# The order of the steps in an attention slot: value products directly behind the scores, all transposes together

## The chip, the cores and the metric

The kernel runs on one core of one Trainium2 chip. The metric is the time of one execution on the device, in microseconds (us). Lower is better. The core has a matrix engine (TensorE, PE in the profile, whose weight loads are listed as PEld), a vector engine (VectorE, DVE), a scalar engine (ScalarE, ACT), a general engine (GpSimd, POOL) and an engine that issues transfers (SyncE, SP). Each engine works through its own list of instructions in order; semaphores hold an instruction until what it needs is there.

## The reference

A threshold attention is followed by a feed-forward layer with squared ReLU. All inputs of the attention are float32; the two weight matrices arrive as float64.

```python
# q, k, v: (8, 8, 576, 64), tau = 0.02
scores = (1.0 / np.sqrt(64)) * np.matmul(q, k.transpose(0, 1, 3, 2))
thresh = np.max(scores, axis=-1, keepdims=True) - tau
scores = np.where(scores >= thresh, scores, -1000000000.0)
scores = scores - np.max(scores, axis=-1, keepdims=True)
attn = np.exp(scores)
attn = attn / (np.sum(attn, axis=-1, keepdims=True) + 1e-09)
attn_out = np.matmul(attn, v)

# (B, H, S, D) -> (B*S, H*D) = (4608, 512); w_in: (512, 2048), w_out: (2048, 512)
x = attn_out.transpose(0, 2, 1, 3).reshape(4608, 512)
h = np.maximum(x @ w_in, 0.0)
out = h * h @ w_out
```

## The kernel before

**Stages.** The attention comes first (0 to about 663 us), then the hidden layer for nine groups of 512 tokens, then the output layer for the same nine groups. Both layers use a fast matrix multiplication of two levels (seven products in place of eight, twice), whose sums of weights are made on GpSimd during the attention. The change touches the attention alone.

**Head pairs and blocks.** Two heads of one batch entry form a pair; there are 32. A pair has 576 queries, in four blocks of 128 and one of 64 (`t` = 0 to 4, `FULL` = 4), which makes 160 blocks in `slots`. In a full block the two heads stand side by side along the free dimension; in the block of 64 they share the partitions, so it has half the work on the other engines.

**The order of the work is written out by hand.** `slot(n)` (lines 558 to 584) is called for n = -3 to 159. Each call issues the next steps of several blocks, as a software pipeline; the order of the calls in it is the order of the instructions on each engine. The steps of one block:

- `ahead(n + 3, 0)` and `ahead(n + 3, 1)`: the scores of block n + 3. The first takes a score buffer from `sc_pool` (two buffers) and makes the last 64 keys' scores of both heads (line 340; nothing for a block of 64 queries). The second makes the main 512 keys' scores, each head on half of the rows of the array (line 355). Below, these two are called K and S.
- `stage` and `second` move the generator `softmax` on: first head's maximum, second head's maximum and threshold (lines 366 and 371), the exponentials (378) for block n + 2; the two selections with their sums (383), the addition of 1e-9 (387), the reciprocal (389) and the normalisation on GpSimd (398) for block n + 1. A block of 64 queries has one head's worth of these, and `second` skips it.
- `turn_part(n - 1, ...)`: the transposes of the weights of block n - 1, in three parts: "w" for the second head's 512 keys (nothing for a block of 64), "W" for the first head's (both line 439, four transposes each, copied out of the matmul banks by ScalarE at lines 441 or 444), and "R" for the remaining 64 keys of both heads (line 414).
- `values_and_load(n - 2)`: the value products of block n - 2 (lines 469 and 474, each head on half of the columns of the array). Below, V. With the last block of a pair it also issues loads of a later pair's values.
- R puts its transpose into the same bank as V's result (the queue `pending`); its copies (lines 418 to 427) take both out on ScalarE, and the result goes to DRAM at the next `ask()`. In the slot where n - 1 is a pair's first block, R also makes the last transpose for the next pair's queries and keys (line 317), with two more copies (320, 321), two small ones on GpSimd (324), and the loads of a further pair on the SP queue.
- `turn_step(n, 0)` and `turn_step(n, 1)`: only in slots where n is a multiple of 5 (and not for the last pair), four transposes of the next pair's queries and four of its keys (line 306, copies at 311 and 309). Below, q and k.
- `sums_step()`: one sum of weights on GpSimd (lines 130 and 133), in slots 35 to about 78 and 111 to 154. Below, Q.
- `fetch` and `convert1` to `convert6`: load and conversion of one piece of a weight matrix, begun in slots 0, 2, ... 30 and 76, 78, ... 106 (`starts`). They are spread over the slots from three before to four after.

**Banks.** The transposes and the value products take their banks of matmul results from one pool, `b_pool`, with two buffers, in turn (lines 888 and 890). A new tile in a buffer waits for the last reader of the tile before. R takes no bank of its own where V has left one in `pending`.

On TensorE a slot before the change is: w, q, V, R, W, K, k, S.

Of the kernel before, what the change touches and what calls it, by code (L numbers as in the profile page):

```python
# [48 lines left out]
def kernel(  # L49
# [26 lines left out]
    B, H, S, D = q.shape  # L76
# [92 lines left out]
    def weight(m):  # L169
        return weight_tile(*chunks[m][0:3])  # L170

    def fetch(m):
        if m is None:
            return
        src = chunks[m][3]
        three = (lambda t: t.rearrange("p (k o) -> p k o", k=4)) if m < 16 else (lambda t: t)
        if src.dtype == FP32:
            nc.sync.dma_start(out=three(weight(m)[:, :]), in_=src)
            return
        raw = sb.tile([P, 2 * WC], I32, tag="raw", bufs=4, name="raw")  # L180
        nc.sync.dma_start(out=three(raw[:, :]), in_=src.bitcast(I32))
        raws[m] = raw
# [10 lines left out]
    def pick(t, k):  # L193
        return t.rearrange("p (n two) -> p n two", two=2)[:, :, k]

    def convert1(m):
        if m not in raws:
            return
        lo, hi = pick(raws[m], 0), pick(raws[m], 1)
        a = pick(sb.tile([P, 2 * WC], I32, tag="a", bufs=2, name="a"), 0)  # L200
        nc.scalar.activation(out=a.bitcast(FP32), in_=hi.bitcast(FP32), func=AF.Abs)
        parts[m] = (lo, hi, a)
        raws.pop(m)

    def convert2(m):
        if m in parts:
            lo = parts[m][0]
            nc.scalar.activation(out=lo, in_=lo.bitcast(U32), func=AF.Copy, bias=0.0, scale=2.0**-29)

    def convert3(m):  # L210
        if m not in parts:
            return
        a = parts[m][2].bitcast(FP32)
        low, high = (0x38000000, 0x47EFFFFF)
        nc.gpsimd.tensor_scalar(
            out=a, in0=a, scalar1=as_float(high), scalar2=as_float(low), op0=ALU.min, op1=ALU.max
        )

    def convert4(m):
        if m not in parts:  # L220
            return
        lo, hi, a = parts[m]
        nc.vector.tensor_scalar(
            out=a, in0=a, scalar1=3, scalar2=0x3FFFFFFF, op0=ALU.logical_shift_left, op1=ALU.bitwise_and
        )

    def convert5(m):
        if m not in parts:
            return
        lo, hi, a = parts[m]  # L230
        nc.vector.scalar_tensor_tensor(
            out=hi, in0=hi, scalar=-(1 << 30), in1=a, op0=ALU.bitwise_and, op1=ALU.bitwise_or
        )

    def convert6(m):
        if m not in parts:
            return
        lo, hi, _ = parts.pop(m)
        nc.gpsimd.tensor_tensor(out=weight(m)[:, :].bitcast(I32), in0=hi, in1=lo, op=ALU.add)
# [47 lines left out]
    def load_v(i):  # L287
        b, hp = pairs[i]
        h = 2 * hp
        va = sb.tile([P, 2, FULL, D], FP32, tag="va", bufs=2, name="va")  # L290
        vd = vdiag[i % 2]
        nc.sync.dma_start(out=va[:, :, :, :], in_=v[b, h : h + 2, 0:MAIN, :].rearrange("j (p t) d -> p j t d", p=P))
        for j in range(2):
            nc.sync.dma_start(out=vd[ds(j * D, D), ds(j * D, D)], in_=v[b, h + j, MAIN:S, :])
        loaded_v[i] = (va, vd)

    def turn(i):

        qn, kn, rn = loaded.pop(i)
        qT = sb.tile([P, S], FP32, tag="qT", bufs=2, name="qT")  # L300
        kT = sb.tile([P, S], FP32, tag="kT", bufs=2, name="kT")
        turning[i] = (qT, kT, rn)
        for nat, to in ((qn, qT), (kn, kT)):
            pt = bank([P, FULL, P], "pqk")
            for t in range(FULL):
                nc.tensor.transpose(pt[:, t, :], nat[:, t, :], ident[:, :])
            flat, to = pt[:, :, :].rearrange("p t m -> p (t m)"), to[:, 0:MAIN]
            if nat is kn:
                nc.scalar.copy(to, flat)
            else:  # L310
                nc.scalar.activation(out=to, in_=flat, func=AF.Identity, scale=qscale[:, :])  # L311
            yield
# [18 lines left out]
    def scores_rest(i, t):  # L331

        sc = sc_pool.tile([P, 3 * BANK], FP32, tag="sc", name="sc")
        if t < FULL:
            qT, _ = turned[i]
            to = sc[:, MAIN:S]
            to = bass.AP(tensor=to.tensor, offset=to.offset, ap=[to.ap[0], [2 * BANK - S, 2], [1, REST]])
            nc.tensor.matmul(to, qT[:, ts(t, P)], kdiag[i % 2][:, :], start=True, stop=True)  # L340
        return sc

    def scores(i, t, sc):

        qT, kT = turned[i]
        m = BLK[t]  # L350
        for k0, n in ((0, MAIN),) if t < FULL else ((0, MAIN), (MAIN, REST)):
            for j in range(2):
                rows = ds(j * D, D)
                to = sc[rows, ds(k0, n)] if t == FULL else sc[:, ds(j * 2 * BANK, n)]
                nc.tensor.matmul(to, qT[rows, ds(t * P, m)], kT[rows, ds(k0, n)], start=True, stop=True)  # L355
# [94 lines left out]
    def turn_part(n, part):  # L450

        if n < 0:
            return
        if n not in rows_of:
            transposes(n)
        rows_of[n][part]()

    def values(i, t):

        wT, wR = weights.pop((i, t)), rests.pop((i, t))  # L460
        va, vd = loaded_v[i]
        n = BLK[t]
        pt = bank([P, 3, P], "pvR")
        pv = pt[:, 0, 0:n]

        for c in range(FULL):
            for j in range(2):
                rows = ds(j * D, D)
                nc.tensor.matmul(  # L469
                    pv[rows, :], va[:, j, c, :], wT[:, j, c, 0:n], start=(c == 0), stop=False, skip_group_check=True  # L470
                )
        for j in range(2):
            rows = ds(j * D, D)
            nc.tensor.matmul(
                pv[rows, :], vd[:, rows], wR[:, 0:n], start=False, stop=True, skip_group_check=True
            )
        pending.append((pt, n, NB * i + t))
# [12 lines left out]
    def turn_step(n, at):  # L490
        i, left = divmod(n - TURN_AT[at], NB)
        i += 1
        if left == 0 and 0 < i < len(pairs):
            if at == 0:
                turns[i] = turn(i)
            next(turns[i])

    def values_and_load(n):

        if n < 0:  # L500
            return
        i, t = slots[n]
        values(i, t)
        if t == NB - 1:
            turned.pop(i), loaded_v.pop(i)
            if i + 2 < len(pairs):
                load_v(i + 2)
# [3 lines left out]
    def stage(n):  # L511
        if n in jobs:
            next(jobs[n], None)

    def second(n):

        if n in jobs and slots[n][1] < FULL:
            next(jobs[n], None)

    def ahead(n, part):  # L520
        if not 0 <= n < len(slots):
            return
        i, t = slots[n]
        if part == 0:
            jobs[n] = scores_rest(i, t)
        else:
            scores(i, t, jobs[n])
            jobs[n] = softmax(i, t, jobs[n])
# [10 lines left out]
    def sums_step():  # L539
        while summing and next(summing[0], 0) == 0:  # L540
            summing.popleft()

    def ask():

        while later:
            to, from_ = later.popleft()
            nc.sync.dma_start(out=to, in_=from_)
# [7 lines left out]
    def begun(n):  # L555
        return starts.get(n)

    def slot(n):

        sums_start(n)  # L560
        ask()
        turn_part(n - 1, "w")
        convert4(begun(n - 3))
        convert3(begun(n - 2))
        stage(n + 2)
        turn_step(n, 0)
        values_and_load(n - 2)
        convert1(begun(n - 1))
        stage(n + 1)
        second(n + 1)  # L570
        turn_part(n - 1, "R")
        second(n + 2)
        sums_step()
        turn_part(n - 1, "W")
        convert6(begun(n - 4))
        stage(n + 2)
        second(n + 2)
        fetch(begun(n + 3))
        convert5(begun(n - 3))
        ahead(n + 3, 0)  # L580
        stage(n + 1)
        turn_step(n, 1)
        ahead(n + 3, 1)
        convert2(begun(n - 1))


    def inner(product, copy, temp, bank, final, tick):
# [297 lines left out]
    with tc.manual_schedule():  # L885
        with ExitStack() as stack:
# [28 lines left out]
            n = len(slots)  # L915
# [95 lines left out]
def as_float(bits):  # L1011
    import struct

    return struct.unpack("<f", struct.pack("<I", bits))[0]
# [30 lines left out]
```

## Time and profile before

| | us |
|---|---|
| median of 6 runs | 1465.87 (1465.35 to 1468.74) |
| the profiled execution | 1465.59 |
| its span | 1463.3 |
| attention: until the first matmul of the hidden layer (line 708) | 662.8 |
| a head pair (five slots) in slots without conversions | 20.00 |

The span is what the trace shows between the first and the last instruction; 2.3 us of the profiled execution's time lie around it. The granted clock of TensorE is full throughout. Times of instructions are given from the start of the span. A row of the trace in order of time has the start, the duration, the engine, the line of the kernel, the operation, what it writes and reads, how many instructions are merged in the row, and in brackets how long the engine was idle before it and what ended that. TensorE's matmul ends are modelled, so the starts of weight loads (PEld) are the firmer marks. A matmul in float32 appears as two, a transpose as one.

### The profile page before, as it was taken

The numbers are of one execution on the slowest core, as the hardware profiler recorded it, in microseconds if no ns is written. First come the engines' busy times: TensorE is split into PE (matmuls) and PEld (weight loads), VectorE is DVE, ScalarE is ACT, GpSimd is POOL, SyncE is SP. The second block draws the span as 40 slices with busy tenths as digits, with TensorE's granted clock in tenths as the row PEclk, the third lists the DMA queues.
The fourth block names the chain that finished last, engine by engine and source line by source line (L and its number), as shares of the span: only waits on it lengthen the run. The fifth ranks groups of instructions, "written<-read, shape, count | busy, mean of one in ns | idle before, by whom it ended". The sixth has DMA issues, their size and how long they took to land. (4 is left out here: it accounts for less than half of the span.)

```text
span 1463.3 us, 35324 instructions
## 1 busy us (share of the span) xinstructions
PE 1435.2 (98%) x12914; PEld 1215.5 (83%) x12914; DVE 1006.7 (69%) x2152; ACT 889.9 (61%) x1792; POOL 1053.1 (72%) x1318
## 2 busy tenths in 40 slices
PE   8999999999999999999999999999999999999998
PEld 5666666666666666669999999999999999999998
DVE  4888766777887667666777877777765666545663
ACT  5888777777887777774766665766553333322330
POOL 3777788878888888773556655566677777777775
PEclk9999999999999999999999999999999999999999
DMA  4444223566442222202433233433984442244411
GB/s 126 105 129 110 64 64 114 163 229 207 123 121 75 55 55 65 64 26 63 145 127 129 92 112 120 145 123 129 387 292 145 144 130 78 89 140 144 145 30 30
DMA packets 212957, 176.90 MB, mean 121 GB/s; under 512 B 99888, under 2 KB 161328, under 8 KB 212784
## 3 DMA queue, kind: packets, MB, share of 16 engines
q1 hardware_dynamic: 210896, 174.09, 38.0%
q8 instruction: 102, 1.67, 0.5%
q10 hardware_dynamic: 1888, 0.56, 0.2%
q14 instruction: 71, 0.58, 0.1%
HBM read 105.12 MB, written 69.47 MB: 119 GB/s over the span
## 5 line engine op out<-in xcount | busy, mean ns | idle before, releaser
L133 POOL TENSOR_TENSOR arena<-arena 128x512 f32<-128x512 f32 (+1 forms) x314 | 376.8, 1223 | 252.4 <-DVE arena L133 212.4
L708 PE MATMUL ph<-arena,w 128*128 128x128 f32 x3528 | 396.6, 275 | 2.1 <-DVE arena L133 1.1
L843 PE MATMUL po<-w,arena 128*128 128x128 f32 x3528 | 396.3, 275 | 2.1 <-ACT arena L622 1.8
L708 PEld LDWEIGHTS ph<-arena,w 128*128 128x128 f32 x3528 | 394.7, 192 | 3.9 <-DVE arena L133 3.5
L843 PEld LDWEIGHTS po<-w,arena 128*128 128x128 f32 x3528 | 394.7, 192 | 3.6 <-ACT arena L622 2.0
L133 DVE TENSOR_TENSOR arena<-ph,arena 128x512 f32<-128x512 f32 x378 | 255.5, 688 | 94.1 <-PE ph L708 53.6
L366 DVE TENSOR_REDUCE arena<-sc 128x1 f32<-128x576 f32 x288 | 217.4, 755 | 127.8 <-PE sc L355 127.6
L383 DVE SCALAR_TENSOR_TENSOR arena<-sc,arena 128x576 f32<-128x576 f32 x288 | 224.5, 813 | 7.2 <-ACT arena L378 6.9
L398 POOL TENSOR_SCALAR arena<-arena 128x576 f32<-128x576 f32 (+1 forms) x320 | 223.6, 709 | 7.4 <-DVE arena L389 3.0
L133 DVE TENSOR_TENSOR arena<-po,arena 128x128 f32<-128x128 f32 x378 | 108.0, 289 | 169.8 <-PE po L843 166.6
L654 ACT COPY c<-arena 128x512 f32<-128x512 f32 (+1 forms) x303 | 172.7, 579 | 61.3 <-DVE arena L130 55.9
L378 ACT ACTIVATE arena<-sc,arena 128x576 f32<-128x576 f32 x288 | 200.7, 747 | 10.6 <-DVE arena L366 6.4
L439 PEld LDWEIGHTS pwT<-ident,arena 128*128 128x128 f32 x1152 | 128.5, 141 | 77.1 <-issue 29.9
L355 PE MATMUL sc<-arena 64*128 64x512 f32 (+2 forms) x768 | 184.5, 571 | 1.1 <-DVE arena L383 0.7
L130 POOL TENSOR_TENSOR arena<-arena 128x512 f32<-128x512 f32 (+1 forms) x138 | 175.0, 1268 | 11.7 <-DMA arena<-xT 2.0
L439 PE MATMUL pwT<-ident,arena 128*128 128x128 f32 x1152 | 180.9, 280 | 1.2 <-ACT arena L311 0.7
L130 DVE TENSOR_TENSOR arena<-arena,c 128x512 f32<-128x512 f32 (+1 forms) x267 | 174.6, 662 | 6.9 <-ACT c L654 6.4
L441 ACT COPY arena<-pwT 128x512 f32<-128x512 f32 x256 | 151.5, 592 | 41.9 <-PE pwT L439 31.7
L469 PE MATMUL pvR<-arena 128*64 128x128 f32 (+1 forms) x2560 | 163.3, 268 | 5.1 <-ACT arena L441 0.7
L469 PEld LDWEIGHTS pvR<-arena 128*64 128x64 f32 x2560 | 127.8, 136 | 34.9 <-issue 20.6
L687 ACT ACTIVATE arena<-arena 128x512 f32<-128x512 f32 x144 | 89.9, 624 | 77.6 <-POOL arena L133 77.6
L622 ACT COPY arena<-po 128x128 f32<-128x128 f32 x63 | 16.7, 265 | 180.1 <-PE po L843 178.1
(56 smaller groups left out, 1155.6 us busy)
## 6 DMA issues: line engine op xcount, KB each, us to landing
g<-arena SPq DMA_DIRECT2D x144, 256.0 KB, 2.0
arena<-g SPq DMA_DIRECT2D x144, 256.0 KB, 4.3
w<-w SPq DMA_DIRECT2D x98, 256.0 KB, 4.8
out_dram<-arena SPq DMA_DIRECT2D x70, 128.0 KB, 2.3
arena<-in_q_dram SPq DMA_DIRECT2D x64, 128.0 KB, 2.7
arena<-in_v_dram SPq DMA_DIRECT2D x32, 256.0 KB, 2.8
arena<-in_moe_w_out_dram SPq DMA_DIRECT2D x16, 512.0 KB, 4.2
xT<-arena SPq DMA_DIRECT2D x128, 64.0 KB, 1.6
```

Source lines behind the costliest of these rows:

```text
L130: e.tensor_tensor(out=out, in0=x, in1=y, op=ALU.subtract)
L133: e.tensor_tensor(out=out, in0=x, in1=y, op=ALU.add)
L355: nc.tensor.matmul(to, qT[rows, ds(t * P, m)], kT[rows, ds(k0, n)], start=True, stop=True)
L366: nc.vector.tensor_reduce(out=nmx[:, j : j + 1], in_=sc[:, ds(at[j], S)], axis=AXIS.X, op=ALU.max, negate=True)
L378: nc.scalar.activation(out=w[:, ts(j, S)], in_=sc[:, ds(at[j], S)], func=AF.Exp, bias=nmx[:, j : j + 1], scale=1.0)
L383: nc.vector.scalar_tensor_tensor(out=w[:, ts(j, S)], in0=sc[:, ds(at[j], S)], scalar=thr[:, j : j + 1], in1=w[:, ts(j, S)], op0=ALU.is_ge, ...
L398: nc.gpsimd.tensor_scalar(out=out, in0=w, scalar1=r, scalar2=1.0, op0=ALU.mult, op1=ALU.mult)
L439: nc.tensor.transpose(pt[:, c, :], w[:, ds(j * (S + REST) + c * P, P)], ident[:, :])
L469: nc.tensor.matmul(pv[rows, :], va[:, j, c, :], wT[:, j, c, 0:n], start=(c == 0), stop=False, skip_group_check=True)
L654: nc.scalar.copy(c, y)
L708: nc.tensor.matmul(to[:, j, :], W_IN[m, k][:, ts(j, P)], of[k][:, m - 1, :], start=(not more and j == 0), stop=True, skip_group_check=True,)
L843: nc.tensor.matmul(to, g[:, j, :], w[:, j, :], start=(not more and j == 0), stop=(j == 3), skip_group_check=True)
```

## The change

The body of `slot` becomes a table of steps by letter, and two strings give their order. The second is the old order. The first is used for a slot in which no piece of a weight matrix is being loaded or converted (`converting(n)` is false): n = -3, -2, 35 to 74 and 111 to 159, 91 of the 163 slots.

```diff
+    ORDERS = ("LXMqVORwYWKEANBCDSeQfFGk", "LwCBXqVFMORYQWAEefDKNkSG")
+
+    def converting(n):
+
+        return any(begun(n - d) is not None for d in range(-1, 5))
+
     def slot(n):
 
         sums_start(n)
-        ask()
-        turn_part(n - 1, "w")
...
-        ahead(n + 3, 1)
-        convert2(begun(n - 1))
+        steps = {
+            "L": lambda: ask(),
+            "w": lambda: turn_part(n - 1, "w"),
...
+            "X": lambda: stage(n + 2),
+            "q": lambda: turn_step(n, 0),
+            "V": lambda: values_and_load(n - 2),
...
+            "M": lambda: stage(n + 1),
+            "O": lambda: second(n + 1),
+            "R": lambda: turn_part(n - 1, "R"),
+            "Y": lambda: second(n + 2),
+            "Q": lambda: sums_step(),
+            "W": lambda: turn_part(n - 1, "W"),
...
+            "E": lambda: stage(n + 2),
+            "e": lambda: second(n + 2),
+            "f": lambda: fetch(begun(n + 3)),
...
+            "K": lambda: ahead(n + 3, 0),
+            "N": lambda: stage(n + 1),
+            "k": lambda: turn_step(n, 1),
+            "S": lambda: ahead(n + 3, 1),
...
+        }
+        for step in ORDERS[converting(n)]:
+            steps[step]()
```

Without the steps of the conversions, the two orders on each engine are:

| engine | old order | new order |
|---|---|---|
| TensorE | w q V R W K k S | q V R w W K S k |
| ScalarE (copies and exponentials) | w q R W exp exp k | q R w W exp exp k |
| VectorE | first maximum, two selections, second maximum, reciprocal | the same |
| GpSimd | addition, threshold, Q, normalisation | addition, threshold, normalisation, Q |
| SP | stores, loads of V and R, fetch | the same |

More of the change, by code (lines that the diff above doesn't have):

```diff
@@ L556, in begun @@
         return starts.get(n)
+    ORDERS = ("LXMqVORwYWKEANBCDSeQfFGk", "LwCBXqVFMORYQWAEefDKNkSG")
+    def converting(n):
+        return any(begun(n - d) is not None for d in range(-1, 5))
     def slot(n):
         sums_start(n)
-        ask()
-        turn_part(n - 1, "w")
[L563 to L582, printed above, removed]
-        ahead(n + 3, 1)
-        convert2(begun(n - 1))
+        steps = {
+            "L": lambda: ask(),
+            "w": lambda: turn_part(n - 1, "w"),
+            "C": lambda: convert4(begun(n - 3)),
+            "B": lambda: convert3(begun(n - 2)),
+            "X": lambda: stage(n + 2),
+            "q": lambda: turn_step(n, 0),
+            "V": lambda: values_and_load(n - 2),
+            "F": lambda: convert1(begun(n - 1)),
+            "M": lambda: stage(n + 1),
[4 more added lines that the diff above has]
+            "W": lambda: turn_part(n - 1, "W"),
+            "A": lambda: convert6(begun(n - 4)),
+            "E": lambda: stage(n + 2),
+            "e": lambda: second(n + 2),
+            "f": lambda: fetch(begun(n + 3)),
+            "D": lambda: convert5(begun(n - 3)),
+            "K": lambda: ahead(n + 3, 0),
+            "N": lambda: stage(n + 1),
+            "k": lambda: turn_step(n, 1),
+            "S": lambda: ahead(n + 3, 1),
+            "G": lambda: convert2(begun(n - 1)),
+        }
+        for step in ORDERS[converting(n)]:
+            steps[step]()
     def inner(product, copy, temp, bank, final, tick):
```

## The prediction

> **What bounds the kernel now.** I read the page's engine totals first, then busy time by stretches, then the order of work in one slot. TensorE is busy nearly throughout, and the attention stage (0 to 663 us) is the only part that the change touches; behind it TensorE runs the two layers without a gap, so whatever attention gains or loses arrives at the end.
>
> ```profile
> PE 1435.2 (98%) x12914; PEld 1215.5 (83%) x12914; DVE 1006.7 (69%) x2152; ACT 889.9 (61%) x1792; POOL 1053.1 (72%) x1318
> ...
> 200.00:240.00 40.00, 39.39 (x370) 26.21 (x366) 27.58 (x65) 28.96 (x63) 32.37 (x55) 1.00 0.24 60
> ```
>
> In this stretch without conversions every engine has room except TensorE, whose matmul ends are modelled. So I go by the starts of its weight loads. One ordinary slot (n mod 5 = 3):
>
> ```profile
> 211.48 0.86 PEld L469 LDWEIGHTS pvR<-arena 128*64 128x64 f32 x16 [0.17 <-issue]
> ...
> 212.73 0.14 PEld L414 LDWEIGHTS pvR<-ident,arena 128*128 128x128 f32 x1 [0.17 <-issue]
> 212.79 0.47 PEld L439 LDWEIGHTS pwT<-ident,arena 128*128 128x128 f32 x4
> ...
> 213.10 0.37 ACT L418 COPY arena<-pvR 128x256 f32<-128x256 f32 x1 [0.87 <-PE pvR L414]
> 213.23 0.30 PEld L340 LDWEIGHTS sc<-arena 128*128 128x128 f32 x2
> ...
> 213.65 0.30 PEld L355 LDWEIGHTS sc<-arena 64*128 64x128 f32 x4
> ...
> 214.71 0.42 PEld L439 LDWEIGHTS pwT<-ident,arena 128*128 128x128 f32 x4 [0.76 <-issue]
> ...
> 215.30 0.86 PEld L469 LDWEIGHTS pvR<-arena 128*64 128x64 f32 x16 [0.17 <-issue]
> ```
>
> The reader sees V (L469) last 1.25 us until R (L414), R 0.06, W 0.44, K 0.42, S (L355) 1.06, w 0.59: 3.82. The w of 0.59 is four transposes (0.44 without a break, as W) and a gap of some 0.17 ahead of V. The slot after it shows the second limit:
>
> ```profile
> 214.83 0.76 DVE L366 TENSOR_REDUCE arena<-sc 128x1 f32<-128x576 f32 x1 [1.39 <-PE sc L355]
> ...
> 215.56 0.82 DVE L383 SCALAR_TENSOR_TENSOR arena<-sc,arena 128x576 f32<-128x576 f32 x1
> ...
> 216.30 0.08 DVE L383 DVE_READ_ACCUMULATOR arena<-sc,arena 128x1 f32 x1
> 216.30 0.81 DVE L383 SCALAR_TENSOR_TENSOR arena<-sc,arena 128x576 f32<-128x576 f32 x1
> ...
> 217.17 0.30 PEld L340 LDWEIGHTS sc<-arena 128*128 128x128 f32 x2
> ```
>
> S (213.65) lets VectorE's maximum start 1.18 later; 0.73 on comes the first selection, 0.74 on the second, and 0.87 after that starts K, which needs the score buffer it frees: 3.52, and with K's 0.42 a ring of 3.94. So S to S takes, for n mod 5 = 0, 1, 2, 3, 4: 4.50, 3.46, 4.28, 3.82, 3.94, together 20.00 a head pair. Only slot 3 and slot 0 are TensorE's; the others go round through VectorE.
>
> **The change, part by part.** It acts in slots -3 and -2 (nearly empty), 35 to 74 and 111 to 159. No instruction is added or removed.
>
> *S directly ahead of V.* The last head pair has no transposes between them in one slot, so the trace prices it: from S (641.53) to V is 1.06, as from S to w. The change thus drops the 0.17 between w and V, where a w exists: four slots in five.
>
> ```profile
> 642.59 0.86 PEld L469 LDWEIGHTS pvR<-arena 128*64 128x64 f32 x16 [0.76 <-ACT arena L378]
> ```
>
> The Trainium skill, "TensorEngine Tiling (Array Packing)", Key Properties, says that changing the tiling mode drains TensorE; the gap of 0.17 agrees. By that rule alone 64 slots would save 0.17 each, 11 us, and the time would be 1454.7.
>
> *w between R and W.* Pool `b` has two banks. Before, the allocations went w, V, W: V's bank was asked for again only by the next w, after K and S. Now they go V, w, W: W takes the bank that R's copy on ScalarE still reads. What such a wait costs is in slot 1, where V takes the bank of k:
>
> ```profile
> 203.27 0.61 ACT L309 COPY arena<-pqk 128x512 f32<-128x512 f32 x1
> ...
> 203.92 0.55 PEld L469 LDWEIGHTS pvR<-arena 128*64 128x64 f32 x16 [0.36 <-ACT arena L309]
> ```
>
> V starts 0.04 after the copy ends. R's copy starts 0.37 after R's load (213.10 less 212.73) and takes 0.37, so W can't start before R + 0.78; w would let it start at R + 0.06 + 0.43 = 0.49. The wait is 0.29, more than the 0.17 saved. Queued behind W on TensorE are K, S and V; on ScalarE, W's copy and then both exponentials, for which the next slot's first selection waits. The Trainium skill, "PSUM — Partial Sum Buffer", on bank collisions, keeps two engines from one bank at one time, whatever the columns; this speaks against the new order.
>
> *The same in slot 1.* There R is followed by the last transpose of q and k, and four copies read the bank: the row below ends 1.17 after R's load (204.66). W starts at R + 1.21 instead of R + 0.60. If W waited only for the columns that it overwrites, up to 0.2 less.
>
> ```profile
> 205.61 0.22 ACT L321 COPY arena<-pvR 128x64 f32<-128x64 f32 x1
> ```
>
> *k behind S.* In slot 0 the 0.59 of k (with its gap) leaves the way from K to S, so slot 0 ends on VectorE's ring; the k transposes then stand ahead of V in slot 1, the shortest slot, whose cover was VectorE. Its copy stays behind the exponentials on ScalarE.
>
> *POOL's sum (Q, 1.27) behind the normalisation (1.48).* Now the next slot's addition of 1e-9 (L387) is queued behind the sum. The threshold ends 0.6 after S (217.90 + 0.31 less 217.59), and 1.48 + 1.27 behind it make POOL free at S + 3.4; the second selection, which the addition needs, ends at S + 3.45. So it is not late, and the reciprocal on VectorE (L389) that waits for it stands behind a second maximum of 0.75 anyway. Price nothing; a lateness of more than some 0.4 would push that reciprocal and with it the next slot's first maximum, each 0.1 by 0.1. The SP queue keeps its order: stores first, R's loads next, fetches (slots -3 and 73 only) last; R's loads wait for k's transposes, now 1 us later, but are needed four slots on.
>
> *New slots, S to S.* ScalarE: w's copy starts at R + 0.84, W's at W + 0.78, the exponentials 0.49 after it (217.41 to 217.90 before) for 1.38, the first selection 0.10 after their end.
> - Slot 2: VectorE. The exponentials of slot 1 end 2.01 after S, selection 2.11, second 2.85, K 0.94 later (as before), S 0.41: 4.20.
> - Slot 3: 1.06 + 1.25 + 0.78 + 0.44 + 0.42 = 3.95, TensorE.
> - Slot 4: also 3.95; exponentials end at S + 1.79, selection 1.89, K at 3.50 against TensorE's 3.53.
> - Slot 0: selection again 1.89, K 3.50, S 3.92 (no w there, so W takes q's bank, long free).
> - Slot 1: 1.06, k 0.59, V 0.74 (64 columns), W at 1.21 more, 0.44 and 0.20: 4.24.
> Differences: -0.08, +0.13, +0.01, -0.58, +0.78: together +0.26 a pair, 20.26.
>
> Slots 35 to 74 and 115 to 154 are 16 pairs: +4.2. Slots 111 to 114: about +0.15; slot 155: +0.04. At the end scores are over and V waits for W's copy (653.27 before); with W late by its wait and its copy behind w's, V to V grows from 2.75 to 3.44. By the same steps V of block 158 moves from 658.77 to 660.31: +1.5. Sum +5.9.
>
> The profiled execution took 1465.59 us (span 1463.3, 2.3 around it); the median of six is 1465.87, so the sum is made against a typical run. Forecast 1465.6 + 5.9 = **1471.5**. Errors of 0.05 in a slot make 0.25 a pair, 4 us: 1467 to 1476 for this case alone.
>
> **Rivals.**
> 1. *W doesn't have to wait* (faster). It decides where R's copy is done 0.43 after R, or W gets another bank. For: TensorE's own work falls. Against: two banks, and the copy ends at 0.74. Then W starts at R + 0.49 and slot 3 takes 3.66 (-0.16); slot 0 -0.58 as above. In the others the exponentials, kept back by w's and W's copies in a row, end 1.88, 2.20 and 1.94 after S: selections 0.10 on, 0.74 and K's 0.87 to 0.94 and 0.41 (no K in slot 1) give 3.62, 4.39 and 4.07 in slots 1, 2 and 4: +0.16, +0.11, +0.13. Together -0.34 a pair, -5.4: 1460.2. Even then most of the removed gap goes to VectorE's ring.
> 2. *The wait is partly covered* (no change). If the copies in slot 1 hold W only column by column, slot 1 costs 4.04 and a pair +0.06; with the tail at +1.5 the sum is +2.5, and 1468.1 stands at the edge of what can be told. For: four separate copies. Against: no row shows a wait that is settled by columns.
> 3. *ScalarE sets the pace* (much slower). If w's and W's copies push the exponentials 0.15 later than I have them, the first selection is late in slots 4, 0, 1 and 2: 0.6 a pair more, +9.6: 1481. For: the maximum's end and the exponentials' end are within 0.05 of each other in slot 4. Against: ScalarE has 11 of 40 us idle in this stretch.
>
> **How the numbers follow.** Forecast 0.56; rival 1 0.13; rival 2 0.16; rival 3 0.15. What a measurement here can tell from no change is about 0.2%, 2.9 us. Slower by more: the forecast's greater part and rival 3, 0.67. Faster by more: 0.13. Within: 0.20. The range of 8 in 10 reaches from 1462, between rivals 1 and 2, to 1479, short of rival 3; it includes the 4 us on either side of the forecast's sum.
>
> **What would show it.** Right: in slots 2 to 4 of the stretches without conversions W's first weight load waits for ScalarE's L418 by about 0.3, 0.04 after its end, and in slot 1 for L321 by 0.6; V starts 1.06 after S; S to S goes 4.50 to 3.92 in slot 0 and 3.46 to 4.24 in slot 1; a pair takes 20.26; stretches with conversions stay at 20.0. Wrong: no such wait (rival 1), or selections waiting for the exponentials by over 0.1 in slots 0 and 4 (rival 3), or a V that starts later than 1.06 after S.

## The result, and the profile after

The changed kernel takes 1469.29 us (median of 19 runs, 1468.45 to 1471.45) against 1465.58 us before (39 runs): a ratio of 1.0025, 95% interval 1.0019 to 1.0031. It is 3.7 us slower. Its profiled execution has a span of 1467.6 against 1463.3.

Busy time in a stretch without conversions is the first view again (length; then busy time and instructions of PE, PEld, DVE, ACT and POOL; clock; share of the DMA engines; GB/s):

```profile
200.00:240.00 40.00, 39.11 (x363) 26.00 (x363) 27.26 (x65) 28.67 (x63) 32.02 (x54) 1.00 0.25 60
```

Every engine does a little less in 40 us than before (TensorE 363 matmuls for 370), so the slots are longer, and no engine has become busier. The order in time tells why. An ordinary slot of the changed kernel (n mod 5 = 3), from S to S:

```profile
210.67 0.30 PEld L355 LDWEIGHTS sc<-arena 64*128 64x128 f32 x4
...
211.73 0.86 PEld L469 LDWEIGHTS pvR<-arena 128*64 128x64 f32 x16 [0.76 <-ACT arena L378]
...
212.98 0.14 PEld L414 LDWEIGHTS pvR<-ident,arena 128*128 128x128 f32 x1 [0.17 <-issue]
213.04 0.47 PEld L439 LDWEIGHTS pwT<-ident,arena 128*128 128x128 f32 x4
...
213.35 0.37 ACT L418 COPY arena<-pvR 128x256 f32<-128x256 f32 x1 [1.82 <-PE pvR L414]
...
213.78 0.42 PEld L439 LDWEIGHTS pwT<-ident,arena 128*128 128x128 f32 x4 [0.26 <-ACT arena L418]
...
214.17 0.30 PEld L340 LDWEIGHTS sc<-arena 128*128 128x128 f32 x2
...
214.59 0.30 PEld L355 LDWEIGHTS sc<-arena 64*128 64x128 f32 x4
```

V stands 1.06 behind S, and the break of 0.17 between w and V is gone. But the second group of L439 (W) starts only 0.06 after R's copy (L418) ends at 213.72: TensorE loaded no weights for 0.26 ahead of it. In slot 1, with the copies of the last rows of q and k, the wait is more than twice that:

```profile
204.63 0.14 PEld L414 LDWEIGHTS pvR<-ident,arena 128*128 128x128 f32 x1
...
205.59 0.22 ACT L321 COPY arena<-pvR 128x64 f32<-128x64 f32 x1
...
205.86 0.42 PEld L439 LDWEIGHTS pwT<-ident,arena 128*128 128x128 f32 x4 [0.59 <-ACT arena L321]
...
206.45 0.20 PEld L355 LDWEIGHTS sc<-arena 64*64 64x64 f32 x4 [0.17 <-issue]
```

The list of waits (engine, line, who was waited for: total us, times, longest) has both as new entries; before, L439's weight loads waited for neither copy:

```profile
PEld pwT L439 <- ACT arena L418: 14.2, 54, 0.3
...
PEld pwT L439 <- ACT arena L321: 10.0, 17, 0.6
```

From S to S, by the first weight load of S in each slot, the slots without conversions compare so (median over slots 120 to 154; "pair" is the whole stretch divided by 7):

| slot, n mod 5 | before | forecast | after |
|---|---|---|---|
| 0 | 4.49 | 3.92 | 3.91 |
| 1 | 3.46 | 4.24 | 4.19 |
| 2 | 4.28 | 4.20 | 4.23 |
| 3 | 3.82 | 3.95 | 3.91 |
| 4 | 3.94 | 3.95 | 3.94 |
| pair | 20.00 | 20.26 | 20.19 |

The difference of the two spans, by the same marks: slots 35 to 74 +1.51, 111 to 114 +0.18, 115 to 154 +1.27, 155 and 156 +0.04, from the last scores to the first weight load of the hidden layer +1.5; against it -0.54 in slots 75 to 110, which run the same order in both. The remaining 0.4 lies ahead of the first scores, which start at 9.7 to 10.8 in the traces of this document, whatever the edit.

### The profile page after: what moved, and what is told of

Same layout as the page of the kernel before. It is cut to its first block, busy times and chain, and to the rows that moved or that the text cites. A ratio compares the mean times of both kernels' runs of the same rounds, so it can differ in the third digit from the quotient of the medians.

```text
span 1467.6 us, 35286 instructions
## 1 busy us (share of the span) xinstructions
PE 1435.9 (98%) x12914; PEld 1215.2 (83%) x12914; DVE 1007.3 (69%) x2152; ACT 890.6 (61%) x1792; POOL 1053.3 (72%) x1318
## 4 chain that ended last, share of the span: by engine, by line
PE 84%; ACT 5%; DVE 5%; POOL 2%; issue 2%; DMA 2%; SPq 0%; ACTq 0%; DVEq 0%; POOLq 0%
PE po L854 27%; PE ph L719 23%; PE sc L355 10%; PE pvR L469 9%; PE pwT L439 7%; PE sc L340 2%; PE pvR L414 2%; DVE arena L383 2%; PE pvR L474 2%; PE pqk L306 2%; ACT arena L378 2%; DVE arena L133 1%; POOL arena L133 1%; DVE arena L366 1%; POOL arena L398 1%
## 5 line engine op out<-in xcount | busy, mean ns | idle before, releaser
L439 PE MATMUL pwT<-ident,arena 128*128 128x128 f32 x1152 | 181.0, 280 | 8.5 <-ACT arena L321 6.0
L439 PEld LDWEIGHTS pwT<-ident,arena 128*128 128x128 f32 x1152 | 128.5, 141 | 60.2 <-ACT arena L418 14.2
```

The costliest lines, as they stand in the source:

```text
L439: nc.tensor.transpose(pt[:, c, :], w[:, ds(j * (S + REST) + c * P, P)], ident[:, :])
```

## The experiments

Each edit is shown against the changed kernel; `...` in place of the second string stands for the old order. Slots that convert weights keep the old order unless it is said otherwise, and where an expectation says "the old order everywhere", the first string is the old order too. A ratio compares with runs of the kernel before on the same chip at the same time, whose median differed a little from chip to chip (1465.1 to 1465.7).

**The parts one by one.** w alone:

```diff
-    ORDERS = ("LXMqVORwYWKEANBCDSeQfFGk", ...
+    ORDERS = ("LCBXqVFMORwYQWAEefDKNkSG", ...
```

> Only w moves behind R; k stays ahead of S and the sum ahead of the normalisation. Theory (W's wait for R's copy costs more than the gap saved; the move of k only carries time from slot 0 to slot 1): slot 0 4.50, slot 1 3.62, slot 2 4.2, slot 3 3.92, slot 4 3.94, a pair 20.2 as with the whole change; with the tail's 1.5 us the time is 1469 to 1470, the whole loss. Rival (k ahead of V in the shortest slot is the loss): a pair at or under 20.0 and at most the tail's loss, 1467 or less.

Measured: 1468.77 us, ratio 1.0025 (1.0015 to 1.0036). Slots 0 to 4: 4.49, 3.61, 4.23, 3.92, 3.94, a pair 20.18. The kernel before took 1465.09 beside it, so the move of w alone costs 3.7 us, the whole loss.

k alone:

```diff
+    ORDERS = ("LwCBXqVFMORYQWAEefDKNSkG", ...
```

> Only k moves, behind S; w stays ahead of V. Theory: slot 0 falls from 4.49 to 3.90; in slot 1 V waits for k's copy, which ends 2.45 after S, so slot 1 grows from 3.46 to about 4.04: a pair 20.0, the tail as before, 1465.6 within 1.5 us. Rival (k's move is the loss): 3 us or more slower than before.

Measured: 1464.36 us, ratio 0.9994 (0.9986 to 1.0003): 3.88, 3.99, 4.34, 3.82, 3.94, a pair 19.96. Slot 0 gives what was expected (0.61), and slots 1 and 2 take nearly all of it back (0.53 and 0.06). In slot 1 it is because V must wait for k's bank:

```profile
202.78 0.61 ACT L309 COPY arena<-pqk 128x512 f32<-128x512 f32 x1
203.43 0.55 PEld L469 LDWEIGHTS pvR<-arena 128*64 128x64 f32 x16 [0.53 <-ACT arena L309]
```

The copy ends at 203.39, V starts 0.04 later: 2.44 after S (200.99), against the 2.45 forecast. The rival, that k's move is the loss, is out.

The sum on GpSimd alone:

```diff
+    ORDERS = ("LwCBXqVFMORYWAEefDKNQkSG", ...
```

> Only the weight sum on GpSimd moves behind the normalisation. Theory: it is covered, 1465.6 within 1 us. Rival (the addition of 1e-9 and the reciprocal come late): slots get longer, 1467 or more.

Measured: 1465.45 us, ratio 1.0004 (0.9995 to 1.0012), a pair 20.00. It is covered.

**The tail.**

```diff
     def converting(n):
-        return any(begun(n - d) is not None for d in range(-1, 5))
+        return n > 155 or any(begun(n - d) is not None for d in range(-1, 5))
```

> The whole change, but slots 156 to 159 keep the old order. Theory: the value products after the last scores are again 2.75 apart in place of 3.43, and the time is 1.5 us under that of the whole change, 1467.8. Rival (a later end of the attention is taken up by waits at the start of the hidden layer): no difference, 1469.3.

Measured: 1468.41 us, ratio 1.0020 (1.0011 to 1.0029). This lies between the theory (1467.8) and the rival (1469.3), and the intervals of this run and of the whole change overlap, so the times alone don't settle it. The traces do. The first weight load of the hidden layer stands 13.92 after S of block 159 before (648.87), 15.39 in the changed kernel (651.73) and 13.92 here (651.71). The rows are in this order; their durations and counts end with the view:

```profile
662.79 5.32 PEld L708 LDWEIGHTS ph<-arena,w 128*128 128x128 f32 x47 [0.44 <-ACT arena L922]
```

```profile
667.12 0.97 PEld L719 LDWEIGHTS ph<-arena,w 128*128 128x128 f32 x8 [0.44 <-ACT arena L933]
```

```profile
665.63 2.53 PEld L719 LDWEIGHTS ph<-arena,w 128*128 128x128 f32 x22 [0.44 <-ACT arena L933]
```

Before, the last value products start 2.75 apart:

```profile
656.02 0.86 PEld L469 LDWEIGHTS pvR<-arena 128*64 128x64 f32 x16 [0.22 <-ACT arena L441]
...
658.77 0.86 PEld L469 LDWEIGHTS pvR<-arena 128*64 128x64 f32 x16 [0.97 <-ACT arena L441]
```

In the changed kernel they start 3.43 apart, because W's copy, which V needs, comes behind R's copy and w's:

```profile
656.23 0.86 PEld L469 LDWEIGHTS pvR<-arena 128*64 128x64 f32 x16 [0.91 <-ACT arena L441]
...
659.66 0.86 PEld L469 LDWEIGHTS pvR<-arena 128*64 128x64 f32 x16 [0.97 <-ACT arena L441]
...
663.09 0.86 PEld L469 LDWEIGHTS pvR<-arena 128*64 128x64 f32 x16 [0.97 <-ACT arena L441]
```

Nothing of it is taken up by the hidden layer: from its first weight load to the end of the span it is 800.4 to 800.5 in all three.

**Is the wait the loss, and what stands behind it?** R's copies read a constant in SBUF in the slots with the new order:

```diff
+    def away(n, part, pt):
+        if converting(n + 1):
+            return pt[:, part, :]
+        return bass.AP(tensor=ident.tensor, offset=ident.offset, ap=[ident.ap[0], [0, 2], [1, P]])[:, part, :]
...
-                nc.scalar.copy(xr[:, :, :], pt[:, 0:2, :])
+                nc.scalar.copy(xr[:, :, :], away(n, slice(0, 2), pt))
```

and likewise for the other copies of R and of the last rows of q and k.

> The whole change, but in its slots R's copies on ScalarE read a constant of the same shape in SBUF in place of the bank, so W need not wait for them; left out are therefore the value products, the last 64 keys' weights and the last rows of q and k. Theory (the wait of W is the loss, and behind it the ring through VectorE and ScalarE holds the slots): W follows w without a gap, slots 0 to 4 take 3.92, 3.62, 4.3, 3.66, 4.07, a pair 19.6, 8 to 9 us under the whole change, 1460 to 1461. Rival A (TensorE alone sets the pace): slots fall to TensorE's own work, 3.8, 3.6, 3.7, 3.7, 3.7, a pair 18.5, 27 us less, 1442. Rival B (the wait costs nothing): no difference from the whole change.

Measured: 1457.87 us, ratio 0.9948 (0.9933 to 0.9963): slots 3.88, 3.65, 4.28, 3.67, 3.99, a pair 19.50. It is 11.4 us under the changed kernel, some 2.5 more than expected: 0.69 a pair over 16 pairs is 11.0, and the forecast had made slots 4 and 0 too long by 0.08 and 0.04. The eight transposes now run together, but slot 2 gains nothing by it. There the first selection waits for the exponentials, the second ends at 208.55, and TensorE loads no weights for 0.53 ahead of K (0.22 in the same slot of the changed kernel):

```profile
207.00 0.82 DVE L391 SCALAR_TENSOR_TENSOR arena<-sc,arena 128x576 f32<-128x576 f32 x1 [0.19 <-ACT arena L386]
...
207.24 0.91 PEld L447 LDWEIGHTS pwT<-ident,arena 128*128 128x128 f32 x8
...
207.74 0.81 DVE L391 SCALAR_TENSOR_TENSOR arena<-sc,arena 128x576 f32<-128x576 f32 x1
...
208.68 0.30 PEld L348 LDWEIGHTS sc<-arena 128*128 128x128 f32 x2 [0.53 <-issue]
```

So rival A (TensorE alone) and rival B (no cost) are both out: without the wait, the order would have gained half a per cent, and no more, because VectorE's ring and the exponentials hold the slots other than slot 3: K or S also waits for VectorE's selection by 0.20 in slot 1 and 0.29 in slot 4, and in slot 0 K starts 0.05 after the selection's end. These copies also read another memory and no longer wait for R, so ScalarE's timing is changed too (R's copy takes 0.40 in place of 0.37, and starts earlier).

The same, but with the two copies of the last rows of q and k again from the bank:

```diff
-            then = turn_last(i + 1, pt[:, 2, :], None if converting(n + 1) else ident[:, :]) if ...
+            then = turn_last(i + 1, pt[:, 2, :]) if ...
```

> As the run in which R's copies read a constant, but the copies of the last rows of q and k (slot 1) read the bank again; left out are the value products and the last 64 keys' weights. Theory: only slot 1 changes against that run: W waits for the last of those two copies, 0.96 behind R, and slot 1 takes 3.9 in place of 3.65, a pair 19.75 in place of 19.50: 1461.7 to 1462. Rival (slot 1's length isn't set by these copies): 1458, as that run.

Measured: 1461.38 us, ratio 0.9969 (0.9958 to 0.9979): slot 1 takes 3.92, a pair 19.72. Of the 0.69 a pair that the waits cost, two copies in one slot hold 0.22.

**Does VectorE's ring set the old slots?** The second head's selection over half the keys, first in the old order, then in the new:

```diff
+            half = 2 if j and not converting(NB * i + t - 1) else 1
             nc.vector.scalar_tensor_tensor(
-                out=w[:, ts(j, S)], in0=sc[:, ds(at[j], S)], scalar=thr[:, j : j + 1], in1=w[:, ts(j, S)],
+                out=w[:, ds(j * S, S // half)], in0=sc[:, ds(at[j], S // half)], scalar=thr[:, j : j + 1], in1=w[:, ds(j * S, S // half)],
```

> The old order everywhere; in slots without conversions the second head's selection covers only the first 288 of 576 keys, about 0.37 us less on VectorE (the other keys' weights stay unselected). Theory (the old slots 1, 2 and 4 go round through VectorE): slot 1 3.25, slot 2 3.9, slot 3 unchanged at 3.82, slot 4 3.82, slot 0 4.43: 0.7 to 0.8 less a pair, 11 to 13 us, 1453 to 1455. Rival (TensorE's own work sets the old slots): no change, 1465.6.

Measured: 1456.49 us, ratio 0.9939 (0.9924 to 0.9953): slots 4.49, 3.37, 4.03, 3.82, 3.82, a pair 19.53. Slots 1, 2 and 4 fall, slots 0 and 3 don't: the rival is out. The fall is 0.47 a pair, not 0.7 to 0.8. The half selection takes 0.52 and lets the next start 0.44 later, a relief of 0.30 and not 0.37, and in slot 2 the first selection waits for the exponentials:

```profile
206.31 0.82 DVE L384 SCALAR_TENSOR_TENSOR arena<-sc,arena 128x576 f32<-128x576 f32 x1 [0.23 <-ACT arena L378]
```

> The same half selection in the new order. Theory (with the wait of W on it TensorE sets slots 1 and 3 and is close in slots 0 and 4, so VectorE's relief is worth less): slot 1 4.19 and slot 3 3.92 unchanged, slot 4 3.92, slot 0 3.82, slot 2 4.0: 0.3 to 0.4 less a pair, 5 to 6 us under the whole change, 1463 to 1464. Rival (the new slots still go round through VectorE everywhere): 0.37 less in each slot but 3, 1.5 a pair, 24 us.

Measured: 1462.96 us, ratio 0.9981 (0.9972 to 0.9991): slots 3.82, 4.19, 3.97, 3.92, 3.92, a pair 19.82, each as expected. The same relief is worth 0.47 in the old order and 0.37 in the new, and nothing at all in slots 1 and 3, which TensorE holds with its new wait.

**A version that beats both.** k's move cost nothing and gained 0.04 a pair, so it was tried in all slots:

```diff
+    ORDERS = ("LwCBXqVFMORYQWAEefDKNSkG", "LwCBXqVFMORYQWAEefDKNSkG")
```

> Only k moves behind S, in all slots, with conversions or without. k alone took 0.04 off a pair where it was tried; over 32 pairs that is 1.3 us: 1464.2. If slots with conversions have less room on ScalarE, nothing is gained: 1465.4.

Measured: 1463.35 us, ratio 0.9986 (0.9977 to 0.9995). Faster, by more than the 0.05 a pair over 32 pairs explains (1.6). In the traces slots -2 to 34 together took 0.85 less than before and slots 75 to 110 took 1.29 less, so the slots that convert weights gain more than the others; why was not looked into. Slot 80, below, was 0.45 shorter, but slot 81 was 0.44 longer.

Slot 80 takes 6.33 before and 5.82 in the changed kernel, where its like take 4.49. In the trace before, R's copy waits for a store of an earlier result, and GpSimd's sum waits beside it for the first input of the hidden layer:

```profile
339.00 1.27 POOL L130 TENSOR_TENSOR arena<-arena 128x512 f32<-128x512 f32 x1 [1.96 <-DMA arena<-xT]
...
339.19 0.37 ACT L418 COPY arena<-pvR 128x256 f32<-128x256 f32 x1 [2.56 <-DMA xT<-arena]
```

Both wait for one queue: the input's four loads (`load_x`, called in slot 76) were issued on SP from 332.40 on, and the last landed at 338.93; the store was issued behind them at 334.92 and landed at 339.11. Only the copy's wait was seen when the next edit was made: more buffers, once in the old order and once with k moved:

```diff
-            xr = sb.tile([P, 2, P], FP32, tag="xr", bufs=3, name="xr")
+            xr = sb.tile([P, 2, P], FP32, tag="xr", bufs=6, name="xr")
```

> The old order everywhere, with six buffers in place of three for the tile that R's copies write. In slot 80 of every run so far R's copy waited 2.0 to 2.6 us for a store of an earlier such tile, which stands on the SP queue behind loads for the hidden layer. With more buffers that wait goes: 1463. If the stall then comes back a few slots later, no change.

Measured: 1466.09 us, ratio 0.9998 (0.9989 to 1.0007). No gain: slot 80 takes 6.23. The copy doesn't wait any more, but GpSimd waits for the loads as long as before (1.94 for 1.96), and behind it wait the reciprocal, a selection and K:

```profile
338.57 1.28 POOL L130 TENSOR_TENSOR arena<-arena 128x512 f32<-128x512 f32 x1 [1.94 <-DMA arena<-xT]
...
340.20 0.17 DVE L389 RECIPROCAL arena<-arena 128x2 f32<-128x2 f32 x1 [2.23 <-POOL arena L387]
...
342.54 0.30 PEld L340 LDWEIGHTS sc<-arena 128*128 128x128 f32 x2 [1.94 <-DVE arena L383]
```

> k behind S in all slots and six buffers for the tile that R's copies write. If both gains hold and add, 1461.7, 0.25% under before; if the second only moves the stall, 1464.

Measured: 1463.40 us, ratio 0.9991 (0.9982 to 0.9999): the buffers add nothing by themselves. The traces of the two runs with six buffers hold one thing more. Behind the stall the granted clock of TensorE was halved, for 3.4 us with the old order (343.96 to 347.37; the row below has the clock as 0.50) and for 6.8 us with k moved (342.7 to 349.5, in an execution of 1466.25 us). Slot 81 took 4.67 and 6.31 there, and 3.57 before. In the trace before, the stall is as long as in the first of the two, and the clock stays full.

```profile
343.96:347.37 3.41, 3.41 (x29) 2.03 (x26) 2.36 (x6) 2.30 (x5) 2.28 (x4) 0.50 0.58 211
```

The last run also begins the sums of that input later:

```diff
-                if n > IN_FIRST + 1 and n % 3 == 0:
+                if n > IN_FIRST + 7 and n % 3 == 0:
```

> k behind S in all slots, six buffers for the tile that R's copies write, and the first sum for the hidden layer's input on GpSimd at slot 84 in place of 78. With six buffers R's copy no longer waited for its store in slot 80, but GpSimd waited 1.9 us for the input's loads and held up the slot as long. If that was the only wait behind the first, slots 80 and 81 fall by 2 to 2.5 us together and the time is 1461; if a third stands behind it, 1463.4.

Measured: 1461.06 us, ratio 0.9967 (0.9955 to 0.9979). Slot 80 takes 3.88 and slot 83, which had been 4.99 before, 3.82. It is faster than both kernels: 4.6 us under before and 8.2 under the changed one. Whether the later sums alone would do was not tried: they were not run with three buffers.

## Why the prediction was right

The forecast was 1471.5 and slower, with a range of 1462 to 1479; measured were 1469.3 and slower. Step by step:

- **S directly ahead of V, 1.06.** Right: 1.06 in the changed kernel, as in the one slot of the old trace that had it.
- **W waits for R's copy.** Right: W starts 0.80 after R where 0.78 was forecast, and in slot 1 1.23 after R where 1.21 was forecast. (The row's 0.26 is counted from the end of w's last weight load, the forecast's 0.29 from where the next would have started, so the two don't measure the same stretch.) That this is the loss was shown by the move of w alone (the whole loss) and by the copies that leave the bank (the loss gone).
- **k carries time from slot 0 to slot 1.** Right: -0.58 and +0.73 in the changed kernel, where slot 1 holds W's wait too, and with k alone -0.61 and +0.53.
- **The sum on GpSimd costs nothing.** Right, shown by its move alone.
- **VectorE's ring.** Right for slots 1, 2 and 4 of the old order, with the half selection. The price of the order without the wait (rival 1) was 19.66 a pair, measured 19.50: the forecast put the exponentials too late, with slots 2 and 4 at 4.39 and 4.07 where they took 4.28 and 3.99.
- **The tail.** +1.5 forecast, 1.47 by the first weight load of the hidden layer.
- **The sum.** +5.9 forecast, +3.7 in the medians; the direction and the mechanism came as forecast, the size was too large. The mis-sized term is the pair: +0.26 forecast, +0.19 measured, 1.1 us over 16 pairs. Most of it lies behind the wait: in slots 1 and 3 the step behind W (S or K) starts 0.05 sooner than forecast once W has waited (K 0.39 after W, from 213.78 to 214.17, where the forecast took the 0.44 of an unbroken group). Slot 117 took 0.27 more than its like before and not after the change; before, its first selection waited 0.47 for the exponentials, and what made them late was not looked into. With that, the stretches that the change touches grew by 4.5 in the traces. The rest, down to 3.7, lies outside the change and can't be told from two traces: slot 80 alone takes 5.6 to 7.0 in ten traces with no edit near it.
- **The rivals.** The first (no wait) failed on two banks, as argued; its mechanism is real, as the copies that leave the bank show. Of the second, slot 1's copies hold W together: W starts behind the last of the four. The third didn't come: in slot 4 the exponentials end at 216.39 and the maximum at 216.53, so ScalarE was just in time.

The Trainium skill, "TensorEngine Tiling (Array Packing)", Key Properties, says that a change of mode drains TensorE. The gap of 0.17 between w and V agrees, though no run here shows what fills it; its saving taken alone would have given 1454.7, by the prediction's estimate. Even with the waits taken away the order came to 1457.9. There slot 3 shows the saving (3.82 to 3.67), but slots 2 and 4, which wait for VectorE, took 4.28 and 3.99 where they took 4.28 and 3.94 before.

## What to carry to other kernels

Before steps are moved together, write down the order in which they take buffers from their pool: with two buffers, a step waits for the last reader of the step before the previous one, and the step between must last as long as that reader. A gap of the matrix engine saved in every slot is worth only what the slot's other ring leaves; here most slots ended on VectorE. When a step is moved from one slot to the next, price both slots, and before a buffer is added to end one wait, look for a second wait that stands beside it.

## What the runs showed of the hardware

- From the first weight load of the main scores (float32, 512 keys, half of the rows of the array) to the first weight load of the next group it took 1.06 us, whether full-array transposes (213.65 to 214.71 before) or value products on half of the columns (210.67 to 211.73 after) came next.
- TensorE's next weight load starts 0.05 us after the end of the copy that held its bank, in all 71 waits of W for R's copies in the changed kernel and in 31 waits of V for k's copy before.
- One burst of loads can hold two engines at once: before, ScalarE waited 2.56 us for a store that was issued behind the loads on the same queue and landed 0.18 after the last of them, while GpSimd waited 1.96 us for the loads themselves. With the first wait removed, the slot was as long as before (6.33 and 6.23).
- The granted clock can fall to half for single stretches of 3.4 or 6.8 us. While it did (342.7 to 349.5 in the trace with k moved and six buffers), the weight loads of successive transposes stood 0.21 us apart; at the full clock they stand 0.11 apart. In the profiled run of the sum on GpSimd alone it was halved from 1068.2 to 1071.6, and from the first weight load of the hidden layer to the end took 802.1 us, against 800.5 before. What brings it on was not tried.
